# Second-half expert products between first-half outputs, and two more weight buffers, in a fused attention and mixture-of-experts kernel

## The chip, the cores and the metric

The kernel runs on one core of a Trainium2 chip, as one program with one launch. The time is that of the device, in microseconds (us). Each number called "median" is over several executions of the same program; the profile is of one execution of its own. A core has TensorE (PE in the profile, with PEld for its weight loads), VectorE (DVE), ScalarE (ACT), GpSimd (POOL) and SyncE (SP). In this kernel SP issues every transfer between the chip's memory and the on-chip buffers, on one in-order queue, and the transfers run on the core's 16 DMA engines.

## What is computed

Attention with a learned relative-position bias is followed by a soft mixture of experts. The sizes are 8 batches, 8 heads, 576 positions, 64 dims per head; then 4608 tokens of 512 features, 8 experts with 4 slots each, hidden size 1024. All is float32.

```python
# attention: q, k, v are (8, 8, 576, 64)
scores = q @ k^T / sqrt(64) + bias        # bias[h, i, j] = relu(x w1 + b1) @ w2,  x = log1p|i-j| / log1p(max(i, 1))
attn   = softmax(scores)                  # over j
x      = (attn @ v) as (4608, 512)
# mixture of experts
logits     = x @ phi                      # (4608, 32 slots)
slot_input = softmax_over_tokens(logits)^T @ x          # (8 experts, 4 slots, 512)
for e in range(8):
    h = maximum(slot_input[e] @ w1[e], 0)               # w1[e]: 512 x 1024
    slot_out[e] = h @ w2[e]                             # w2[e]: 1024 x 512
out = softmax_over_slots(logits) @ slot_out             # (4608, 512)
```

The expert weights are 8 x 512 x 1024 for w1 and as many for w2. The kernel cuts them into 64 tiles of 512 KB: 32 of w1, then 32 of w2. The result is 9 MB.

## The kernel before

**Main part.** There are 32 units: four pairs of heads (`hp`), and for each pair the eight batches. A bias stage of about 54 us comes first and writes the position bias to memory; each unit then computes scores, softmax and the product with v. In the last pair of heads (units 24 to 31) each unit also does its share of the token mixing (`moe`). The order of all this work is written out by hand: `PLAIN` gives each step of the early units a place, `END` lists the steps from unit 22 on, and every engine runs its instructions in the order in which they were recorded.

**Weights.** `worder` fixes the order of the 64 tiles: tiles 0 to 31 are w1; tiles 32 to 47 are the first half of w2's output columns (`hf` = 0), with two groups `Q` of four experts (32 to 39 and 40 to 47); tiles 48 to 63 are the second half, again with two groups (48 to 55 and 56 to 63). `fetch_w(home)` loads the next tile in this order into a buffer of the pool and tag that is its `home`. The pool `wp` has `W1N` = 24 buffers of 4 KB per partition. During the two middle pairs of heads, each unit fetches one or two tiles into `wp`, by this line:

```python
step(u, "wf", lambda _, u=u: fetch_w((wp, "w"), 2 if u < B + W1N - 2 * B else 1))
```

With B = 8 that is two tiles in units 8 to 15 and one in units 16 to 23, 24 in all. In the last unit, steps named `w21` to `w36` fetch tiles into buffers that attention no longer needs: the bias buffers (`bm`), the query/key buffers (`qk`), the score buffers (`y`), the transposed-attention buffers (`at0`, `at1`), and `v`, `xo`, `xt`, `xk`. After the main part 44 tiles have been asked for. The remaining 20 take over a buffer whose tile has been used; `refetch(i, ...)` asks for the next tiles into the homes of tiles i.

**The end.** After the last unit the code runs straight on, and these are the steps that the change touches:

- `turn_slots` turns the slot inputs, and makes `sel`, two 128 x 128 selection matrices.
- `first(j)`, j = 0 to 7, multiplies the slot inputs by four w1 tiles; `hidden` and `turn_hidden` apply the relu and transpose.
- `second(hf, Q)` multiplies by eight w2 tiles: 32 matmuls (line 888). It holds one of the four pairs of PSUM banks from the call with Q = 0 until the call with Q = 1 has been copied out to `so`.
- `gather_slots(hf)` moves the expert results into the order of the slots (line 899) and copies them to `sst` (line 903).
- `put(hf, b)` makes the output of batch b for half of the columns: four matmuls (line 921) into two bank pairs, one copy on DVE and one on ACT into `ob` (line 315), and a 512 KB transfer by SP (line 924). After every fourth b a rest of 256 KB follows (lines 929, 932, 933).

The order at the end of the code is this, and it is also the order in which PE and SP do it:

```python
gather_slots(0)
for b in range(8):
    put(0, b)
for Q in range(2):
    second(1, Q)
gather_slots(1)
for b in range(8):
    put(1, b)
```

Of the kernel before, what the change touches and what calls it, by code (L numbers as in the profile page):

```python
# [10 lines left out]
F32 = mybir.dt.float32  # L11
F32R = mybir.dt.float32r
AF = mybir.ActivationFunctionType
ALU = mybir.AluOpType
# [2 lines left out]
DRAM = bass.MemoryType.DRAM  # L17


W1N = 24  # L20
W2N = 5
AHEAD = 3
JB0 = 32
# [102 lines left out]
def body(ctx, tc, qk, v, wcol, phi, mw1, mw2, tabh, consth, out, outr):  # L126
    nc = tc.nc
    P = 128
# [8 lines left out]
    const = ctx.enter_context(tc.tile_pool(name="const", bufs=1))  # L137
    dram = ctx.enter_context(tc.tile_pool(name="dram", bufs=1, space=DRAM))
    psp = ctx.enter_context(tc.tile_pool(name="psp", bufs=1, space=PSUM))
    wp = ctx.enter_context(tc.tile_pool(name="wp", bufs=W1N))  # L140
    ldp = ctx.enter_context(tc.tile_pool(name="ldp", bufs=2))
# [3 lines left out]
    xp = ctx.enter_context(tc.tile_pool(name="xp", bufs=1))  # L145
# [16 lines left out]
    rsum = const.tile([P, P], F32, name="rsum")  # L162
# [3 lines left out]
    et2 = xp.tile([P, 256], F32, name="et2", tag="et2")  # L166
# [23 lines left out]
    rowm = cons[:, NJ:]  # L190
# [20 lines left out]
    for g in range(4):  # L211
        rs = slice(32 * g, 32 * g + 32)
        nc.vector.tensor_scalar(out=wbd[rs, H * g:H * g + H], in0=cols[rs, 2:2 + H], scalar1=1.0 / QS, scalar2=None,
                                op0=ALU.mult)
# [99 lines left out]
    def cp(eng, out, in_):  # L314
        (nc.vector.tensor_copy if eng else nc.scalar.copy)(out=out, in_=in_)  # L315
# [22 lines left out]
    def then(u, names, f):  # L338

        place, eng = max(rank[u, n] if (u, n) in rank else (5 * u + PLAIN[n][0], PLAIN[n][1]) for n in names.split())  # L340
        prog.append((place, len(prog), lambda: f(eng)))
# [415 lines left out]
    def fetch_w(home, n=1):  # L757
        for _ in range(n):
            i = nw[0]
            nw[0] += 1  # L760
            w, e, c, hf = worder[i]
            homeof.append(home)
            if not free:
                pool, tag = home
                if tag == "v":
                    free.append([pool.tile([P, 512], F32, name="wt", tag=tag) for _ in range(2)])
                else:
                    x = pool.tile([P, 2, 2, 512] if tag in twice else [P, 1, 2, 512], F32, name="wt", tag=tag)
                    free.extend(x[:, i] for i in range(x.shape[1]))
            wt = free.pop(0)  # L770
            if w == 1:
                nc.sync.dma_start(out=wt, in_=mw1[e, c * P:(c + 1) * P, :].rearrange("p (x d) -> p x d", x=2))
                wt = [wt[:, n, :] for n in range(2)]
            else:
                src = mw2[e, c, hf]
                if type(wt) is list:
                    for n in range(2):
                        nc.sync.dma_start(out=wt[n].rearrange("p (x d) -> p x d", x=2), in_=src[:, 2 * n:2 * n + 2, :])
                else:
                    nc.sync.dma_start(out=wt.rearrange("p y (x d) -> p (y x) d", x=2), in_=src)  # L780
                    wt = [wt[:, n, :] for n in range(2)]
            wtiles[i] = wt
# [12 lines left out]
    for u, (hp, b) in enumerate(units):  # L795
# [9 lines left out]
        if 1 <= hp < NP - 1:  # L805
            step(u, "wf", lambda _, u=u: fetch_w((wp, "w"), 2 if u < B + W1N - 2 * B else 1))
        if u == 1:
# [9 lines left out]
    then(U - 1, "w34 M0.4 M1.4", lambda _: fetch_w((ldp, "v")))  # L817
    then(U - 1, "w34 K01 K23 KR L", lambda _: fetch_w((xp, "xo")))
    then(U - 1, "w34 K01 K23 KR L", lambda _: fetch_w((xp, "xt")))
    sel = [const.tile([P, P], F32, name=f"sel{i}") for i in range(2)]  # L820
    csts, ends, hT2 = {}, {}, {}

    def refetch(*ids):
        for i in ids:
            fetch_w(homeof[i])

    def turn_slots():
        nc.vector.tensor_scalar(out=stS, in0=stS, scalar1=1e-9, scalar2=None, op0=ALU.add)
        nc.vector.reciprocal(out=stS, in_=stS)
        h = Banks()  # L830
        nc.tensor.transpose(out=h.t[:, 0, 0:P], in_=accs, identity=ident)
        sT = ends["sT"] = xp.tile([P, 4, 32], F32, name="sT", tag="ek", bufs=2)
        nc.scalar.copy(out=sT, in_=h.read()[:, 0, 0:P].rearrange("a (c s) -> a c s", c=4))
        for Q in range(2):
            nc.vector.tensor_scalar(out=sel[Q], in0=rsum, scalar1=rowm[:, Q:Q + 1], scalar2=None, op0=ALU.mult)

    def first(j):

        Q, kc = j // 4, j % 4
        if kc == 0:  # L840
            ends["h", Q] = Banks(2)
        for n in range(2):
            for g in range(4):
                nc.tensor.matmul(ends["h", Q].t[32 * g:32 * g + 32, n, :], ends["sT"][:, kc, :], wtiles[4 * j + g][n],
                                 start=kc == 0, stop=kc == 3, tile_position=(0, 32 * g))
# [32 lines left out]
    def second(hf, Q):  # L878

        if Q == 0:  # L880
            ends["o"] = Banks(2)
            ends["so"] = so if hf else wp.tile([P, 2, 512], F32, name="so", tag="w")
        po = ends["o"].t[:, Q, 0:256]
        for fq in range(2):
            for x in range(4):
                for g in range(4):
                    i = 32 + 16 * hf + 8 * Q + 4 * fq + g
                    nc.tensor.matmul(po[32 * g:32 * g + 32], hT2[Q][:, 4 * fq + x, 32 * g:32 * g + 32],  # L888
                                     wtiles[i][x // 2][:, 256 * (x % 2):256 * (x % 2) + 256], start=fq == 0 and x == 0,
                                     stop=fq == 1 and x == 3, tile_position=(0, 32 * g))  # L890
        ends["o"].read()
        cp(Q == 0, ends["so"][:, hf, 256 * Q:256 * Q + 256], po)
        return ends["so"]

    def gather_slots(hf):
        h = Banks()
        pf = h.t[:, 0]
        for Q in range(2):
            nc.tensor.matmul(pf[:, 0:256], sel[Q], so[:, hf, 256 * Q:256 * Q + 256], start=Q == 0, stop=Q == 1)
        h.read()  # L900
        if hf == 0:
            ends["sst"] = wp.tile([P, DM], F32, name="sst", tag="w")
        nc.scalar.copy(out=ends["sst"][:, 256 * hf:256 * hf + 256], in_=pf[:, 0:256])
# [3 lines left out]
    def put(hf, b):  # L907

        sst = ends["sst"][:, 256 * hf:256 * hf + 256]
        pool, tag, n = homes2[8 * hf + b]  # L910
        if n == 0:
            ob = pool.tile([P, 4, 256], F32, name="ob", tag=tag)
        else:
            if n == 1:
                obs[tag] = pool.tile([P, 2, 4, 256], F32, name="ob", tag=tag)
            ob = obs[tag][:, n - 1]
        for z in range(2):
            h = Banks()
            for y in range(2):
                rs = slice(32 * (2 * z + y), 32 * (2 * z + y) + 32)  # L920
                nc.tensor.matmul(h.t[:, y, 0:256], ends["cT"][rs, b, :], sst[rs], start=True, stop=True,  # L921
                                 tile_position=(32 * (2 * z + y), 0))
            cp(z == 0, ob[:, 2 * z:2 * z + 2, :], h.read()[:, :, 0:256])
        nc.sync.dma_start(out=out[b, hf], in_=ob.rearrange("p c d -> p (c d)"))
        if b % 4 == 3:
            h = Banks()
            for r in range(4):
                rs = slice(32 * r, 32 * r + 32)
                nc.tensor.matmul(h.t[64 * (r % 2):64 * (r % 2) + 64, r // 2, 0:256], ends["cR"][rs, b // 4, :], sst[rs],
                                 start=True, stop=True, tile_position=(32 * r, 64 * (r % 2)))  # L930
            obr = wp.tile([P, 2, 256], F32, name="obr", tag="w")
            nc.scalar.copy(out=obr, in_=h.read()[:, :, 0:256])
            nc.sync.dma_start(out=outr[b // 4, hf], in_=obr)
# [4 lines left out]
    with tc.manual_schedule():  # L938
        for _, _, f in sorted(prog, key=lambda x: x[:2]):
            f()  # L940
        turn_slots()
        for j in range(4):
            first(j)
            refetch(*range(4 * j, 4 * j + 4))
        hidden(0)
        first(4)
        first(5)
        turn_hidden(0)
        first(6)
        refetch(24, 25, 27)  # L950
        first(7)
        refetch(28)
        hidden(1)
        so = second(0, 0)
        turn_hidden(1)
        stack(0)
        second(0, 1)
        stack(1)
        gather_slots(0)
        for b in range(8):  # L960
            put(0, b)
        for Q in range(2):
            second(1, Q)
        gather_slots(1)
        for b in range(8):
            put(1, b)

# [61 lines left out]
```

## Time and profile before

| What | Value |
|---|---|
| Median of three runs | 609.73 us (607.46 to 612.27) |
| The profiled execution, its time | 607.81 us |
| The profiled execution, its span from first to last instruction | 605.4 us |
| What lies around the span | 2.4 us |
| Mean granted TensorE clock | 0.993 |
| PE busy | 582.2 us, 96% of the span |
| Moved by DMA | 110.73 MB, 183 GB/s over the span |

The times in the views are microseconds from the start of the span. "Idle before" names what released an engine that had been waiting. A view of windows gives, for each stretch, the busy time of each engine, the granted clock, the share of time that the 16 DMA engines were busy, and what they moved; a share of a little over 1 means that all 16 were busy throughout. An SP row in the view of the timeline shows when transfers were issued, not when their bytes moved. The profile's lines themselves stand in the prediction, where they are used.

### The profile page before, as it was taken

How to read it: one execution, taken by the hardware profiler on the slowest of the kernel's cores; microseconds unless marked ns; L12 is line 12 of the kernel's file. 1: busy time of each engine (PE TensorE's matmuls, PEld its weight loads, DVE VectorE, ACT ScalarE, POOL GpSimd, SP SyncE). 2: the span in 40 equal slices, each digit the busy share in tenths (PEclk: the TensorE clock that was granted, in tenths of full speed). 3: DMA queues.
4: the chain of work that ended last, by engine and by line, in shares of the span. 5: the costliest groups of instructions: out<-in, count | busy, mean ns of one | idle time of the engine just before them, and what ended most of it. 6: DMA issues, size and time to landing. Idle time of an engine off the chain costs nothing.

```text
span 605.4 us, 18911 instructions
## 1 busy us (share of the span) xinstructions
PE 582.2 (96%) x7423; PEld 370.5 (61%) x7423; DVE 414.9 (69%) x1320; ACT 469.8 (78%) x974; POOL 224.6 (37%) x336
## 2 busy tenths in 40 slices
PE   6998899999999999999999999999999999999993
PEld 4874666666666666666666666665666666653551
DVE  7997767667676667667676667677679788852233
ACT  6996888888888888888888888887877887751233
POOL 0001644455555544455555544544233422400000
PEclk9999899999999999999999999999999999999998
DMA  6778222333855544675444356522332145689997
GB/s 223 272 243 298 66 84 84 109 101 123 242 183 190 174 156 154 216 251 175 138 156 138 120 203 222 164 75 73 123 123 71 55 129 210 207 331 324 410 381 316
DMA packets 41897, 110.73 MB, mean 183 GB/s; under 512 B 7120, under 2 KB 7248, under 8 KB 41808
## 3 DMA queue, kind: packets, MB, share of 16 engines
q1 hardware_dynamic: 41808, 109.52, 53.2%
q8 instruction: 58, 0.95, 0.7%
q14 instruction: 31, 0.25, 0.1%
HBM read 82.10 MB, written 27.41 MB: 181 GB/s over the span
## 4 chain that ended last, share of the span: by engine, by line
PE 83%; DMA 6%; DVE 4%; ACT 3%; issue 1%; POOL 0%; SPq 0%; DVEq 0%; ACTq 0%; POOLq 0%
PE ps L473 25%; PE ps L370 21%; PE ps L348 17%; PE ps L260 7%; PE ps L366 6%; DMA wt<-in_moe_w_dram 5%; ACT y L390 2%; PE ps L539 1%; DMA xo<-xs 1%; PE ps L669 1%; PE ps L888 1%; DVE ob L315 1%; PE ps L921 1%; DVE y L383 0%; POOL y L312 0%
## 5 line engine op out<-in xcount | busy, mean ns | idle before, releaser
L312 POOL TENSOR_SCALAR y<-y,sm 128x576 f32<-128x576 f32 (+1 forms) x320 | 221.9, 707 | 302.1 <-DVE sm L399 246.6
L383 DVE CUSTOM_DVE_ANT_0 y<-ps,bm 128x576 f32<-128x576 f32 x256 | 185.3, 754 | 95.5 <-PE ps L348 55.2
L390 ACT ACTIVATE y<-y,mn 128x576 f32<-128x576 f32 x288 | 222.1, 772 | 28.3 <-DVE sm L398 19.3
L315 ACT COPY at<-ps 128x1024 f32<-128x1024 f32 (+3 forms) x211 | 153.9, 732 | 37.0 <-PE ps L348 28.3
L473 PE MATMUL ps<-at,v 128*64 128x320 f32 (+1 forms) x1280 | 176.4, 415 | 0.0
L370 PE MATMUL ps<-qk 64*128 64x288 f32 x1024 | 155.6, 421 | 0.1
L348 PEld LDWEIGHTS ps<-ident,y 64*128 64x128 f32 x2624 | 103.1, 139 | 56.5 <-POOL y L312 16.0
L348 PE MATMUL ps<-ident,y 64*128 64x64 f32 x2624 | 118.0, 226 | 4.1 <-POOL y L312 3.6
L473 PEld LDWEIGHTS ps<-at,v 128*64 128x64 f32 x1280 | 84.0, 137 | 60.7 <-issue 10.8
L370 PEld LDWEIGHTS ps<-qk 64*128 64x128 f32 x1024 | 90.8, 188 | 26.7 <-DVE sm L398 9.8
L390 ACT ACTIVATION_READ_ACCUMULATOR y<-y,mn 128x1 f32 x288 | 53.9, 187 | 0.0
L260 PE MATMUL ps<-f,wbd 128*32 128x79 f32 (+32 forms) x856 | 48.4, 345 | 1.7 <-DVE f L239 1.6
L239 DVE TENSOR_SCALAR f<-tabs,scl,nb 128x576 f32<-128x576 f32 (+17 forms) x114 | 47.9, 496 | 0.5 <-DMA tabs<-in_tab_dram 0.5
L315 DVE COPY at<-ps 128x256 f32<-128x256 f32 (+3 forms) x77 | 33.8, 442 | 15.3 <-PE ps L348 13.8
L260 PEld LDWEIGHTS ps<-f,wbd 128*32 128x32 f32 x856 | 33.2, 112 | 16.9 <-issue 8.1
L366 PE MATMUL ps<-qk 64*64 64x288 f32 x256 | 38.0, 415 | 0.0
L315 DVE COPY xts<-ps 128x256 f32<-128x256 f32 (+1 forms) x57 | 25.9, 455 | 12.1 <-PE ps L473 12.1
L264 ACT ACTIVATE e<-ps,bcon 128x591 f32<-128x591 f32 x36 | 26.7, 754 | 4.7 <-DMA bias_m<-e 2.1
L399 DVE RECIPROCAL sm<-sm 128x2 f32<-128x2 f32 (+1 forms) x160 | 26.5, 165 | 5.5
L398 DVE TENSOR_SCALAR sm<-sm 128x2 f32<-128x2 f32 (+1 forms) x160 | 28.3, 177 | 2.9 <-ACT y L390 2.3
L383 DVE CUSTOM_DVE_ANT_0 y<-ps,br 128x576 f32<-128x576 f32 x32 | 24.0, 750 | 1.9 <-PE ps L348 1.1
L383 DVE DVE_READ_ACCUMULATOR2_ANT mn<- 128x1 f32 x288 | 24.1, 84 | 0.0
(144 smaller groups left out, 333.5 us busy)
## 6 DMA issues: line engine op xcount, KB each, us to landing
wt<-in_moe_w_dram SPq DMA_DIRECT2D x63, 512.0 KB, 6.1
qk<-in_qk_dram SPq DMA_DIRECT2D x32, 608.0 KB, 3.8
v<-in_v_dram SPq DMA_DIRECT2D x32, 320.0 KB, 3.2
bias_m<-e SPq DMA_DIRECT2D x32, 295.5 KB, 4.2
out_dram<-ob SPq DMA_DIRECT2D x16, 512.0 KB, 5.9
xs<-xts SPq DMA_DIRECT2D x24, 288.0 KB, 4.9
xo<-xs SPq DMA_DIRECT2D x8, 864.0 KB, 5.4
bm<-bias_m SPq DMA_DIRECT2D x16, 288.0 KB, 4.4
```

What stands on the lines that cost most here:

```text
L239: nc.vector.tensor_scalar(out=f, in0=tabs[:, 0:n], scalar1=scl[:, sc:sc + 1], scalar2=nb1[:, 0:1], op0=ALU.mult, op1=ALU.max)
L260: nc.tensor.matmul(pb[32 * t:32 * t + 32, c0 // 512, c0 % 512:(c1 - 1) % 512 + 1], wbd, x, start=True, stop=True, tile_position=(0, 32 * t))
L264: nc.scalar.activation(out=e, in_=pb.rearrange("a x n -> a (x n)")[:, 0:S + 15], func=AF.Identity, bias=bc)
L312: nc.gpsimd.tensor_scalar(out=out, in0=y, scalar1=r, scalar2=1.0, op0=ALU.mult, op1=ALU.mult)
L315: (nc.vector.tensor_copy if eng else nc.scalar.copy)(out=out, in_=in_)
L348: nc.tensor.matmul(out, src[rs], ident[rs, rs], is_transpose=True, start=True, stop=True, tile_position=(64 * r, 0))
L366: nc.tensor.matmul(pss[0].t[rs, n, 0:HALF], x[rs, 1152:1216], x[rs, 64 + n * HALF:64 + (n + 1) * HALF], start=True, stop=True, tile_positi ...
L370: nc.tensor.matmul(pss[hh].t[:, n, 0:HALF], x[rs, 640 + p * P:640 + (p + 1) * P], x[rs, k0:k0 + HALF], start=True, stop=True, tile_positio ...
L383: nc.vector.tensor_tensor_reduce(out=d["y", p][:, hs].rearrange("a (x n) -> a x n", x=2), in0=t[:, :, 0:HALF], in1=biases[hp][p][:, hs].re ...
L390: nc.scalar.activation(out=y, in_=y, func=AF.Exp, bias=d["mn", p][:, hh:hh + 1], scale=-1.0, accum_out=d["sm", p][:, hh:hh + 1])
L398: nc.vector.tensor_scalar(out=r, in0=r, scalar1=1e-9, scalar2=None, op0=ALU.add)
L473: nc.tensor.matmul(po[64 * hh:64 * hh + 64], d["v"][:, v0:v0 + 64], main[:, :, 4 * hh + i, :] if i < 4 else rest, start=i == 0, stop=i == ...
```

## The change

`W1N` goes from 24 to 26, so `wp` has two more buffers of 4 KB per partition. By the line above, units 16 and 17 now fetch two tiles each instead of one. Since tiles are taken in a fixed order, each later home holds a tile two places further on. After the main part 46 tiles have been asked for, and 18 are left for `refetch` instead of 20; these now go to the homes of tiles 0 to 13 and 16 to 19, all in `wp`. To make room on chip, `sel` moves from buffers of its own into the buffer `et2`, which the mixing steps no longer use by then.

At the end, the two calls of `second(1, Q)`, and `gather_slots(1)`, move from behind the eight first-half outputs to places between them.

```diff
-W1N = 24
+W1N = 26
...
-    sel = [const.tile([P, P], F32, name=f"sel{i}") for i in range(2)]
...
+        sel = ends["sel"] = xp.tile([P, 2, P], F32, name="sel", tag="et2")
         for Q in range(2):
-            nc.vector.tensor_scalar(out=sel[Q], in0=rsum, scalar1=rowm[:, Q:Q + 1], scalar2=None, op0=ALU.mult)
+            nc.vector.tensor_scalar(out=sel[:, Q], in0=rsum, scalar1=rowm[:, Q:Q + 1], scalar2=None, op0=ALU.mult)
...
-            nc.tensor.matmul(pf[:, 0:256], sel[Q], so[:, hf, 256 * Q:256 * Q + 256], start=Q == 0, stop=Q == 1)
+            nc.tensor.matmul(pf[:, 0:256], ends["sel"][:, Q], so[:, hf, 256 * Q:256 * Q + 256], start=Q == 0, stop=Q == 1)
...
         for j in range(4):
             first(j)
-            refetch(*range(4 * j, 4 * j + 4))
+            refetch(*range(4 * j, 4 * j + (4 if j < 3 else 2)))
         hidden(0)
         first(4)
+        refetch(*range(16, 20))
         first(5)
         turn_hidden(0)
         first(6)
-        refetch(24, 25, 27)
         first(7)
-        refetch(28)
         hidden(1)
...
         gather_slots(0)
-        for b in range(8):
+        for b in range(2):
             put(0, b)
-        for Q in range(2):
-            second(1, Q)
+        second(1, 0)
+        for b in range(2, 4):
+            put(0, b)
+        second(1, 1)
+        for b in range(4, 6):
+            put(0, b)
         gather_slots(1)
+        for b in range(6, 8):
+            put(0, b)
         for b in range(8):
             put(1, b)
```

The first place is PE's queue at the end of the program, from the first output on. `wt` is a weight tile, `hT` the transposed hidden values, `so` the expert results, `sst` the results by slot, `cT` and `cR` the combining weights. Before:

```order
L921 MATMUL ps<-sst,cT 128x256 x16
L929 MATMUL ps<-sst,cR 64x256 x4
L921 MATMUL ps<-sst,cT 128x256 x16
L929 MATMUL ps<-sst,cR 64x256 x4
L888 MATMUL ps<-wt,hT 32x256 x64
L899 MATMUL ps<-so,sel_981 128x256
L899 MATMUL ps<-so,sel_982 128x256
L921 MATMUL ps<-sst,cT 128x256 x16
```

And the same queue with the change, from the same first output:

```order
L921 MATMUL ps<-sst,cT 128x256 x8
L888 MATMUL ps<-wt,hT 32x256 x32
L921 MATMUL ps<-sst,cT 128x256 x8
L929 MATMUL ps<-sst,cR 64x256 x4
L888 MATMUL ps<-wt,hT 32x256 x32
L921 MATMUL ps<-sst,cT 128x256 x8
L899 MATMUL ps<-so,sel 128x256 x2
L921 MATMUL ps<-sst,cT 128x256 x8
L929 MATMUL ps<-sst,cR 64x256 x4
L921 MATMUL ps<-sst,cT 128x256 x16
```

The 64 matmuls of line 888 are split in two and now stand behind the second and the fourth output, the gather stands behind the sixth, and the second half's outputs (the last row) follow straight on the first half's.

The second place is SP's queue in unit 16, in the third pair of heads, and unit 17 has the same edit. `qk` and `v` are the loads for the next unit, and `xs` the store of a unit's result.

```order
 L284 DMA qk<-in_qk_dram 128x1216
 L289 DMA v<-in_v_dram 128x640
-L772 DMA wt<-in_moe_w_dram 128x1024
+L772 DMA wt<-in_moe_w_dram 128x1024 x2
 L485 DMA xs<-xts 128x576
```

One more load of 512 KB stands ahead of the unit's store.

The third place is the end of SP's queue; the rows with `wt` are weight loads, `out_dram` the results.

```order
 L780 DMA wt<-in_moe_w_dram 128x1024 x5
 L778 DMA wt<-in_moe_w_dram 128x512 x2
-L780 DMA wt<-in_moe_w_dram 128x1024 x24
+L780 DMA wt<-in_moe_w_dram 128x1024 x22
 L924 DMA out_dram<-ob 128x1024 x4
 L933 DMA out_dram<-obr 128x512
```

Two loads of 512 KB fewer stand ahead of the first output; the order of the outputs among themselves is the same.

## The prediction

> **What bounds the kernel now.** I read the page first, part 4 (the chain that ended last) and the slices of part 2.
>
> ```profile
> span 605.4 us, 18911 instructions
> PE 582.2 (96%) x7423; PEld 370.5 (61%) x7423; DVE 414.9 (69%) x1320; ACT 469.8 (78%) x974; POOL 224.6 (37%) x336
> ...
> PE   6998899999999999999999999999999999999993
> ...
> DMA  6778222333855544675444356522332145689997
> ...
> PE 83%; DMA 6%; DVE 4%; ACT 3%; issue 1%; POOL 0%; SPq 0%; DVEq 0%; ACTq 0%; POOLq 0%
> ```
>
> PE is busy nearly everywhere and is 83% of the chain. Only in the last five slices, some 75 us, are the DMA engines as busy as PE. The change is at this end, so I cut it into windows next.
>
> ```profile
> core 0: us, PE busy (x) PEld busy (x) DVE busy (x) ACT busy (x) POOL busy (x), PEclk, DMA share, GB/s
> 546.00:550.00 4.00, 3.06 (x29) 0.94 (x32) 2.08 (x10) 0.49 (x2) 0.00 (x0) 1.00 0.79 268
> 550.00:560.00 10.00, 10.00 (x96) 3.48 (x92) 1.44 (x2) 1.27 (x2) 0.00 (x0) 1.00 1.01 364
> 560.00:573.00 13.00, 12.81 (x187) 7.15 (x176) 3.16 (x5) 2.23 (x6) 0.00 (x0) 1.00 1.02 409
> 573.00:581.00 8.00, 6.89 (x89) 3.67 (x93) 5.15 (x8) 5.67 (x11) 0.00 (x0) 1.00 1.03 411
> 581.00:588.00 7.00, 7.00 (x126) 4.06 (x118) 0.42 (x1) 0.59 (x2) 0.00 (x0) 1.00 1.03 413
> 588.00:589.00 1.00, 0.84 (x4) 0.30 (x2) 0.00 (x0) 0.21 (x2) 0.00 (x0) 1.00 0.74 295
> 589.00:590.00 1.00, 0.69 (x12) 0.67 (x16) 0.00 (x0) 0.25 (x1) 0.00 (x0) 1.00 0.41 164
> 590.00:591.00 1.00, 0.55 (x15) 0.15 (x8) 0.85 (x2) 0.89 (x2) 0.00 (x0) 1.00 0.19 74
> 591.00:592.00 1.00, 1.00 (x16) 0.52 (x16) 0.74 (x2) 0.44 (x2) 0.00 (x0) 1.00 0.31 125
> 592.00:603.00 11.00, 4.25 (x52) 2.03 (x48) 3.57 (x6) 4.40 (x8) 0.00 (x0) 0.89 1.01 402
> 603.00:604.00 1.00, 0.00 (x0) 0.00 (x0) 0.00 (x0) 0.00 (x0) 0.00 (x0) 0.50 0.49 188
> ```
>
> From 550 to 588 all 16 DMA engines are busy, at 409 GB/s. Between 588 and 591 they run dry one after another (shares 0.74, 0.41, 0.19): the first is done at 588, the last only at about 591. From 592 they are full again until 603.5. The timeline tells what stands where.
>
> ```profile
> start us, us, engine line op out<-in xcount [idle before <-releaser]
> 573.27 1.15 PE L921 MATMUL ps<-sst,cT 32*128 32x256 f32 x16 [0.46 <-ACT sst L903]
> ...
> 574.83 2.95 SPq L924 DMA_DIRECT2D out_dram<-ob  x4
> ...
> 576.31 0.66 PE L929 MATMUL ps<-sst,cR 32*64 32x256 f32 x8 [0.18 <-DVE ob L315]
> ...
> 576.90 2.86 PE L921 MATMUL ps<-sst,cT 32*128 32x256 f32 x32
> ...
> 580.54 7.11 PE L888 MATMUL ps<-wt,hT 128*32 128x256 f32 x128
> ...
> 587.58 1.26 PE L899 MATMUL ps<-so,sel 128*128 128x256 f32 x4
> ...
> 588.14 0.30 PEld L899 LDWEIGHTS ps<-so,sel 128*128 128x128 f32 x2 [0.26 <-ACT so L315]
> ...
> 589.30 1.15 PE L921 MATMUL ps<-sst,cT 32*128 32x256 f32 x16 [0.46 <-ACT sst L903]
> ...
> 590.91 2.99 SPq L924 DMA_DIRECT2D out_dram<-ob  x4
> ```
>
> So the end has two runners. DMA drains weights, then 4.72 MB of first-half outputs (8 x 524,288 + 2 x 262,144 bytes; 11.5 us at 409 GB/s). PE makes the eight first-half outputs until 580.54, then the second half's products, gather and first output, issued at 590.91. DMA runs dry at about the moment at which PE has new outputs. After that it is DMA alone: 590.91, plus 0.8 until bytes move (row 591 to 592), plus 4.72 MB at 402 GB/s = 11.74, is 603.45, where the rows end (0.49 of the window from 603).
>
> **The change part by part.** *Two more buffers.* Units 16 and 17 each load one more tile.
>
> ```profile
> 273.66 0.57 SPq L772 DMA_DIRECT2D wt<-in_moe_w_dram  x1
> ...
> 287.28 0.42 SPq L772 DMA_DIRECT2D wt<-in_moe_w_dram  x1
> ...
> 280.00:300.00 20.00, 20.00 (x224) 12.52 (x222) 13.56 (x48) 17.55 (x37) 8.78 (x14) 1.00 0.40 122
> ```
>
> Each costs SP about 0.5 us and DMA 1.3 us, where DMA is 0.40 busy and PE, which bounds, is full. What queues behind it on SP is the unit's `xs` store, issued 0.5 us later and read only in the last pair of heads. Cost: 0, covered by PE; if that cover were gone, 2.6 us. At the end, 2 x 524,288 bytes are no longer there to be moved between 550 and 588: at 409 GB/s, DMA is through with the weights 2.56 us earlier. For PE that gains nothing before the first output:
>
> ```profile
> ACT hS L850 <- PE ps L844: 11.5, 2, 8.9
> ...
> PE ps L844 <- ACT sT L833: 0.9, 1, 0.9
> ...
> PEld ps L844 <- DMA wt<-in_moe_w_dram: 0.3, 1, 0.3
> ```
>
> Between 546 and 574 others wait for PE, and PE waited for a weight tile for 0.3 us in all. So the first output still starts at 573.27 (bound of the gain: 0.3 us; I take 0). `sel` in another buffer: the same two DVE instructions at the same place, 0.
>
> In the bias stage the same pool holds features and results, and 26 buffers may spare waits there.
>
> ```profile
> ACT e L264 <- DMA bias_m<-e: 2.1, 2, 1.9
> ...
> 20.00:30.00 10.00, 10.00 (x203) 8.16 (x203) 10.00 (x28) 9.50 (x17) 0.00 (x0) 1.00 0.82 290
> ```
>
> ACT waited 2.1 us for a store to leave a buffer, but PE and DVE are full there, so the gain lies between 0 and 2.1 us; I take 0, since the row with PE and DVE at 10.00 of 10 is the nearer one.
>
> *The reordering.* All of PE's work stays; only its order changes. From 573.27:
> - Outputs 0 and 1: four outputs take 576.31 - 573.27 = 3.04, so two take 1.5: 574.8.
> - Second product, group 0: half of 7.11 = 3.55: 578.35.
> - Outputs 2 and 3 (1.5) and a rest (0.6, from 576.31 to 576.90): 580.45. Now the product holds a bank pair, so three instead of four circulate. PE already waits for copies at outputs:
>
> ```profile
> PEld ps L921 <- DVE ob L315: 3.8, 8, 0.8
> ...
> PEld ps L921 <- ACT sst L903: 1.7, 2, 0.9
> ```
>
>   One such wait more costs 0 to 0.8, mean 0.48 (3.8 over 8); I take 0.3, since part of it overlaps with the rest's matmuls: 580.75.
> - Group 1: 3.55: 584.3. In the end 0.4 to 0.5 us of waiting at `so` and `sst` vanishes, since outputs now stand around the gather.
> - Output 4 is issued 1.6 after its first matmul (590.91 - 589.30): 585.9. Its bytes move at 586.7.
>
> DMA's side of it: the slowest engine ends the first half at 591.0 before, so it ended the weights at 579.5; now at 576.9. Outputs 0 and 1 take 2.56: 579.5. Output 2 is issued at 578.35 + 1.6 = 579.95, moves at 580.75: DMA stands for 1.25. Outputs 2, 3 and a rest, 3.2: 583.95. Then nothing until output 4 at 586.7: DMA stands for 2.75. From there it must move outputs 4 to 7 and a rest (2.36 MB, 5.8) and the second half (11.74). PE keeps ahead of it: gather 1.0, and output 6 is issued at 588.4, the second half's first at about 590.5, both before DMA gets to them (589.3 and 592.5). End: 586.7 + 5.8 + 11.74 = 604.2, against 603.45.
>
> The sum: -2.56 (two tiles) - 0.7 (the old hole, 591.0 to 591.7) + 1.25 + 2.75 (two new holes) = **+0.75 us**. It hangs on one path: PE's work until output 4, since all that lies behind it is DMA at full rate. That makes it robust: had the weights not come earlier, the holes would shrink by as much. On the profiled execution's own span that is 606.15, on its time 608.6. That execution stands 1.9 below the median of the runs; on the median, 609.73 + 0.75 = 610.5.
>
> [...]
>
> By the rows, the reordering fills one hole and opens two, because DMA, at 1.28 us an output, has no reserve of outputs while PE does 3.55 us of products.
>
> **The rivals.** *Faster: no new holes.* If DMA lagged far enough behind, it would stay busy from the weights' end (576.9) for 23.2 us to 600.1. That is 3.3 us less: 606.4. For it speaks that SP's issues in the first half are backed up behind full engines; against it that outputs 2 and 4 cannot be issued before 579.95 and 585.9 by PE's rows.
>
> *Slower: the last weights are late.* PE now asks for tiles 56 to 63 at 580.75 instead of 584.1.
>
> ```profile
> L780 SPq DMA_DIRECT2D wt<-in_moe_w_dram x28: 327/328/1459, 532.5 to 570.4; - x28
> ...
> DMA to landing us min/median/max: 3.7/10.1/12.2
> ```
>
> Before, the last was issued at 570.4 and landed at 580.5 to 582.6; less 2.56 that is 578 to 580, just in time. If it lands no earlier than before, PE stands up to 1.85 us there with every later output behind it: 610.5 + 1.85 = 612.3. It decides from a landing after 580.75 on.
>
> *Faster at the front.* The bias stage gives its 2.1 us: 608.4.
>
> **How the numbers follow.** Forecast 0.55; no new holes 0.2; late weights 0.15; bias stage 0.1. All four lie within 6.1 us of 609.73. The range goes down to the first rival's end and up to the second's, with 0.7 more there because the three runs themselves lie 4.8 us apart: 606.4 to 613.0. Faster or slower by over 1%, about what a measurement of this kernel can tell from no change, means under 603.6 or over 615.8. All gains together (3.3 + 2.1 + 0.3) stay below 6.1 and the slower rival adds 2.6, so I leave 0.03 for each side and 0.94 for within.
>
> **What would show it.** In the changed profile: the last wait for weights gone or unchanged up to 573; the product of line 888 in two pieces, at about 574.8 and 580.75; output issues of the first half in pairs at about 574.8, 580, 586 and 588.4; two dips of the DMA share, near 580 and, deeper, from 584 to 586.7, and none around 590; last bytes at about 604. It would be wrong if PE reached output 4 by 584, or if DMA stayed full through 586, or if the span moved before 546, where nothing but two loads is changed after the bias stage.

## The result and the profile after

| | before | after |
|---|---|---|
| Median, measured in turn | 608.28 us (605.81 to 612.27, 20 runs) | 611.55 us (609.47 to 617.27, 20 runs) |
| Ratio, with its 95% interval | | 1.0062 (1.0041 to 1.0083) |
| The profiled execution, time and span | 607.81 and 605.4 us | 612.70 and 610.9 us |
| Mean granted TensorE clock of that execution | 0.993 | 0.984 |
| First output's first matmul to the end of the span ("tail") | 32.17 us | 34.96 us |

The change made the kernel a little slower in this comparison: 0.4 to 0.8%, which is 2.5 to 5.0 us. (A second comparison of the same two kernels, below, gave 1.0021 with an interval from 0.9988 to 1.0054.) The forecast was +0.75, and 611.55 lies in its range of 606.4 to 613.0.

The page of the changed kernel, the same rows as of the kernel before:

```profile
span 610.9 us, 18917 instructions
...
PE 584.7 (96%) x7423; PEld 373.8 (61%) x7423; DVE 414.3 (68%) x1320; ACT 469.8 (77%) x974; POOL 223.8 (37%) x336
...
PE   6998899999999999999999999999999999989992
...
DMA  6778222334765544676544366531332045699967
...
PE 89%; DVE 4%; ACT 2%; issue 2%; POOL 1%; DMA 1%; SPq 0%; DVEq 0%; POOLq 0%; ACTq 0%
```

The work is the same (PE has 7423 matmuls in both). The last slices differ: PE's last digit was 3 and is 2, DMA's last two were 97 and are 67. DMA has a gap in the second slice from the end, and is still at work in the last one.

The first output now starts at 575.95 instead of 573.27, so 2.68 us came in ahead of the part that the prediction is about, and 34.96 - 32.17 = 2.79 us behind it. The two have different causes. The windows of the start of the program, first of the kernel before:

```profile
50.00:60.00 10.00, 8.19 (x93) 4.69 (x90) 6.07 (x19) 6.16 (x12) 1.47 (x2) 1.00 0.92 335
60.00:70.00 10.00, 8.13 (x92) 5.71 (x90) 8.44 (x29) 8.57 (x18) 5.38 (x10) 0.91 0.34 100
70.00:80.00 10.00, 10.00 (x102) 6.03 (x101) 6.95 (x25) 7.44 (x16) 4.38 (x6) 0.92 0.12 43
```

And of the changed kernel:

```profile
50.00:60.00 10.00, 8.20 (x96) 4.45 (x86) 6.12 (x17) 6.71 (x14) 1.47 (x2) 0.97 1.00 358
60.00:70.00 10.00, 7.89 (x70) 5.27 (x71) 6.27 (x23) 5.99 (x13) 3.37 (x6) 0.67 0.35 105
70.00:80.00 10.00, 10.00 (x114) 6.95 (x112) 7.14 (x25) 8.21 (x17) 6.45 (x10) 0.85 0.01 2
```

The column behind POOL is the granted clock. Between 60 and 70 us it is 0.91 before and 0.67 after, and PE did 92 and 70 matmuls there. In these two traces the clock is either full or half: in the kernel before it was half from 68.2 to 71.6, in the changed one from 59.3 to 66.2 and from 69.6 to 73.0, stretches of 3.4, 6.8 and 3.4 us. In both it is half once more at the end, from 600.7 and from 602.0 on, where PE's last matmul ended at 596.8 and at 599.6. What sets the earlier stretches is not shown: between 50 and 70 us PE's longest pause is 1.8 us in the kernel before and 2.1 in the changed one. That the one profile has one stretch of 3.4 us there and the other three (6.8 us counted as two) is not the change's doing, as the experiments below show.

Behind the first output the path is the one that was forecast. The timeline of the changed kernel (start, duration, engine, line):

```profile
575.95 1.15 PE L921 MATMUL ps<-sst,cT 32*128 32x256 f32 x16 [0.46 <-ACT sst L903]
...
577.50 3.66 PE L888 MATMUL ps<-wt,hT 128*32 128x256 f32 x64 [0.40 <-DVE ob L315]
577.51 6.83 SPq L924 DMA_DIRECT2D out_dram<-ob  x4
...
581.09 1.13 PE L921 MATMUL ps<-sst,cT 32*128 32x256 f32 x12
...
582.64 0.70 PE L921 MATMUL ps<-sst,cT 32*128 32x256 f32 x4 [0.42 <-DVE ob L315]
...
583.86 3.66 PE L888 MATMUL ps<-wt,hT 128*32 128x256 f32 x64
...
584.61 0.33 SPq L933 DMA_DIRECT2D out_dram<-obr  x1
...
587.45 1.26 PE L921 MATMUL ps<-sst,cT 32*128 32x256 f32 x16
...
588.96 3.54 SPq L924 DMA_DIRECT2D out_dram<-ob  x4
```

The product of line 888 stands in two pieces, 1.55 and 7.91 us behind the first output's first matmul (forecast 1.53 and 7.48), and output 4 is issued 13.01 behind it (12.63). Windows of the same stretch; the last two columns are the DMA share and GB/s:

```profile
575.95:577.00 1.05, 1.05 (x16) 0.72 (x16) 0.24 (x1) 0.24 (x1) 0.00 (x0) 1.00 0.43 172
577.00:581.00 4.00, 3.60 (x68) 1.98 (x64) 1.04 (x2) 0.83 (x2) 0.00 (x0) 1.00 0.68 266
581.00:583.00 2.00, 1.58 (x20) 0.99 (x16) 1.53 (x3) 0.59 (x1) 0.00 (x0) 1.00 0.06 25
583.00:587.00 4.00, 4.00 (x72) 2.14 (x72) 0.18 (x1) 1.17 (x2) 0.00 (x0) 1.00 0.82 326
587.00:589.50 2.50, 2.26 (x31) 1.37 (x24) 1.29 (x2) 1.45 (x3) 0.00 (x0) 1.00 0.04 9
589.50:600.00 10.50, 9.23 (x107) 4.87 (x105) 6.45 (x10) 7.61 (x14) 0.00 (x0) 1.00 0.99 391
600.00:606.00 6.00, 0.00 (x0) 0.00 (x0) 0.00 (x0) 0.26 (x1) 0.00 (x0) 0.67 1.02 401
606.00:607.00 1.00, 0.00 (x0) 0.00 (x0) 0.00 (x0) 0.00 (x0) 0.00 (x0) 0.50 0.96 377
```

The two holes are there (share 0.06 and 0.04), and from 589.5 on DMA runs full to the end. A third hole, which the prediction does not have, lies ahead of them (share 0.43 in the first row, and 0.68 in the second). By the trace's records the last weight landed 2.3 us behind the first output's first matmul, against 7.15 in the kernel before; the prediction's sum has 3.6. So from about 576.3 to 578.3, until the first output's bytes move, most engines stand idle. The end has something new too. The window that follows in the changed kernel:

```profile
607.60:609.10 1.50, 0.00 (x0) 0.00 (x0) 0.00 (x0) 0.00 (x0) 0.00 (x0) 0.50 0.07 27
```

For 1.5 us the share is 0.07, and one engine of 16 is 0.0625: fifteen engines are done and one still moves bytes, while the whole kernel waits for it. The window in the same place of the kernel before, whose engines all finish between 603.4 and 603.8:

```profile
603.80:605.40 1.60, 0.00 (x0) 0.00 (x0) 0.00 (x0) 0.00 (x0) 0.00 (x0) 0.50 0.02 5
```

### The profile page after: what moved, and what is told of

It reads as the page before. It is cut to its first block, busy times and chain, and to the rows that moved or that the text cites. A ratio compares the mean times of both kernels' runs of the same rounds, so it can differ in the third digit from the quotient of the medians.

```text
span 610.9 us, 18917 instructions
## 1 busy us (share of the span) xinstructions
PE 584.7 (96%) x7423; PEld 373.8 (61%) x7423; DVE 414.3 (68%) x1320; ACT 469.8 (77%) x974; POOL 223.8 (37%) x336
## 4 chain that ended last, share of the span: by engine, by line
PE 89%; DVE 4%; ACT 2%; issue 2%; POOL 1%; DMA 1%; SPq 0%; DVEq 0%; POOLq 0%; ACTq 0%
PE ps L473 25%; PE ps L370 21%; PE ps L348 17%; PE ps L260 7%; PE ps L366 6%; PE ps L888 2%; PE ps L844 2%; PE ps L539 1%; ACT y L390 1%; PE ps L669 1%; PE ps L921 1%; DVE y L383 1%; DVE ob L315 1%; POOL y L312 1%; DMA tabs<-in_tab_dram 1%
## 5 line engine op out<-in xcount | busy, mean ns | idle before, releaser
L370 PEld LDWEIGHTS ps<-qk 64*128 64x128 f32 x1024 | 92.4, 191 | 26.5 <-DVE sm L398 9.8
L260 PE MATMUL ps<-f,wbd 128*32 128x79 f32 (+31 forms) x856 | 48.4, 348 | 2.2 <-DVE f L239 2.1
L315 DVE COPY at<-ps 128x256 f32<-128x256 f32 (+3 forms) x77 | 33.8, 442 | 16.0 <-PE ps L348 14.7
```

The lines of the kernel that those rows point to most:

```text
L260: nc.tensor.matmul(pb[32 * t:32 * t + 32, c0 // 512, c0 % 512:(c1 - 1) % 512 + 1], wbd, x, start=True, stop=True, tile_position=(0, 32 * t))
L370: nc.tensor.matmul(pss[hh].t[:, n, 0:HALF], x[rs, 640 + p * P:640 + (p + 1) * P], x[rs, k0:k0 + HALF], start=True, stop=True, tile_positio ...
```

## The experiments

All kernels are compared by the tail, from the first matmul of the first output to the end of the span, since what is ahead of it moves with the clock (the first output starts between 572.1 and 579.0 us in these profiles). "Last bytes" and other offsets count from the same matmul. Medians of several runs stand beside it where they were taken.

**Which part of the change costs the time.** One part each, the changed kernel again, and a variant in which the bias stage has its old number of buffers.

The buffers alone, in the old order of the end (`W1N`, `sel` and `refetch` as in the change):

```diff
-W1N = 24
+W1N = 26
```

> The two more buffers alone, with the old order at the end. Theory T (the loss lies in the tail, behind the first output): the DMA engines are through with the weights some 2.5 us earlier, the hole before the second half's first output grows by as much, and the end stays where PE puts it: no change against the kernel before, within 0.5 us; from the first output's first matmul to the end of the span 32.1 us, as before. Theory F (the loss lies in the front: 26 instead of 24 buffers change the bias stage or the clock's start): 1.5 to 3 us slower than before, all of it ahead of 80 us.

Measured: 609.45 us, ratio 1.0019 (0.9987 to 1.0051); tail 32.34, last bytes 30.61 (before 32.17 and 30.49).

The order alone, with 24 buffers:

```diff
         gather_slots(0)
-        for b in range(8):
+        for b in range(2):
+            put(0, b)
+        second(1, 0)
+        for b in range(2, 4):
+            put(0, b)
+        second(1, 1)
+        for b in range(4, 6):
             put(0, b)
-        for Q in range(2):
-            second(1, Q)
         gather_slots(1)
+        for b in range(6, 8):
+            put(0, b)
```

> The new order alone, with 24 buffers and the old loads. Theory T: slower than before by 0.75 us (the step to output 4) up to 2.8 us (what the tail of the changed kernel took more in its profile, 34.95 against 32.13 us from the first output's first matmul), more if group 1's weights are late. Theory F: no more than 0.75 us slower, and nothing moved ahead of 546 us.

Measured: 609.21 us, ratio 1.0005 (0.9966 to 1.0044); tail 34.94.

The changed kernel once more, beside the others:

> The changed kernel once more, for a second profile and its clock. Theory T: the tail from the first output's first matmul is again 34 to 35 us. Theory F: the tail is 33 us, 0.75 over the kernel before, and the first output again starts over 575 us with a granted clock under 0.99. If the shift of the front in the first profile (2.7 us) was the clock's chance, it is gone here.

Measured: 610.38 us, ratio 1.0021 (0.9988 to 1.0054); tail 34.92.

The changed kernel, but with the two new buffers under a tag of their own, so that the pool of the bias stage stays at 24:

```diff
-W1N = 26
+W1N = 24
...
+            if u in (16, 17):
+                step(u, "wf", lambda _: fetch_w((wp, "wx")))
```

> The changed kernel with the two more buffers under a tag of their own, so that the bias stage rotates through 24 as before; loads and order at the end as in the changed kernel. Theory T: as slow as the changed kernel, 3 to 3.5 us over the one before. Theory F: the front's part is gone, 0.75 us over the one before.

Measured: 609.49 us, ratio 0.9997 (0.9965 to 1.0029); tail 34.92.

What follows: the tail separates the kernels without overlap. The old order has 32.17 and 32.34, the new one 34.96, 34.94, 34.92 and 34.92, with 24 or 26 buffers. So by these profiles, one or two of each kernel, the change's cost behind the first output is 2.75 to 2.79 us, all of it the order's, and the buffers give nothing there, as forecast ("had the weights not come earlier, the holes would shrink by as much"). The third hole isn't there in the order alone, with 24 buffers, and the tail is as long. The start of the first output lies anywhere from 572.9 to 579.0 in the four profiles of the new order, and 579.0 is the one with the old number of buffers; with the new buffers and the old order it is 573.1. So the 2.68 us at the front of the changed kernel's profile are not the buffers'.

The times of whole runs do not confirm the 2.75 us. They would be a ratio of 1.0045. The interval of the changed kernel reaches beyond that, but those of the other two new orders end at 1.0044 and 1.0029, a little below. In the kernel before, 35 runs on the chip of these four lie between 605.51 and 617.06, so the chance of the front is larger than the effect. The fastest runs do not settle it either: 605.51 before, but 607.20 with the buffers alone in the old order, and 607.84, 608.76 and 607.87 in the three new orders, each out of a third as many runs. The split of the cost rests on the tails.

**Where the holes come from.** Both products ahead of all outputs, which takes the waiting for PE out of the middle and puts it in one piece at the start:

```diff
         gather_slots(0)
-        for b in range(2):
-            put(0, b)
         second(1, 0)
-        for b in range(2, 4):
-            put(0, b)
         second(1, 1)
-        for b in range(4, 6):
+        for b in range(8):
             put(0, b)
         gather_slots(1)
-        for b in range(6, 8):
-            put(0, b)
```

> Both second products ahead of all first-half outputs, none behind one. Theory L (the end is set by the last output that stands behind the second product of group 1: its issue, 0.9 us to the first bytes, then DMA at full rate for all that follows): the first output is issued 8.7 us after the place where it was issued 1.56 us after; all 23.2 us of outputs follow, so from that place to the end of the span 34.6 us, and 36.2 if a 16 KB instruction load falls into it and one DMA engine ends 1.6 us late, as in the changed kernel. Rival S (splitting the outputs is what costs, each product between them a fixed price): no output is split off, so 32.2, as before.

Measured: 609.90 us in one run. The first output starts later here, so the tail is taken from the gather ahead of it: 36.43, against 33.77 before and 36.51 to 36.55 in the changed kernel. The windows of this kernel show the DMA engines empty while PE makes products and the first output:

```profile
573.00:579.80 6.80, 6.80 (x128) 3.90 (x121) 0.42 (x1) 0.24 (x1) 0.00 (x0) 1.00 0.21 83
579.80:582.00 2.20, 1.96 (x32) 1.25 (x29) 1.29 (x2) 1.45 (x3) 0.00 (x0) 1.00 0.00 0
582.00:606.10 24.10, 12.28 (x142) 6.32 (x140) 9.02 (x14) 10.79 (x19) 0.00 (x0) 0.86 0.99 392
584.80:585.20 0.40, 0.32 (x6) 0.27 (x8) 0.40 (x2) 0.30 (x1) 0.00 (x0) 1.00 0.34 133
```

From 582 on DMA is full but for one short dip (the last row), and no engine ends late. A 16 KB load fell at 582.3, ahead of this dip. In the other kernels the first output starts 1.60 behind the gather, so on the scale of the tail 36.43 is 34.83; counted from the product's first matmul (572.76) it is 35.4. Either is near the 34.6 expected, and the 32.2 falls. The long hole costs 36.43 - 33.77 = 2.66 us, about as much as the holes of the changed kernel and its late engine together.

The products later, behind the fourth and the sixth output, so that DMA has a reserve of outputs while PE multiplies:

```diff
         gather_slots(0)
-        for b in range(2):
+        for b in range(4):
             put(0, b)
         second(1, 0)
-        for b in range(2, 4):
-            put(0, b)
-        second(1, 1)
         for b in range(4, 6):
             put(0, b)
+        second(1, 1)
+        put(0, 6)
         gather_slots(1)
-        for b in range(6, 8):
-            put(0, b)
+        put(0, 7)
```

> The second products behind the fourth and the sixth output, so that two first-half outputs stand behind group 1 instead of four. Theory L: the seventh output is issued 13.8 to 14.2 us after the first output's first matmul, then 3.2 and 11.7 us of transfers: span end at 31.4 to 31.8 us, 0.4 to 0.8 less than before the change; 33.0 to 33.4 with a late DMA engine. Rival S: as in the changed kernel, 34.9, since as many products stand between outputs.

Measured: 609.57 us in one run; tail 34.18, last bytes 32.35. A gain of 0.74 to 0.78 us over the changed kernel, less than the 1.5 to 1.9 expected of the places alone: output 6 is issued 14.50 behind the first matmul, and output 7 only 1.65 later, because the gather stands between. The window in which this shows:

```profile
587.00:589.00 2.00, 2.00 (x24) 1.09 (x20) 0.69 (x1) 1.02 (x3) 0.00 (x0) 1.00 0.05 18
```

**The bank pair.** The prediction gave 0.3 us to the product's hold on one of four bank pairs while outputs 2 and 3 are made. Here each of the two calls takes a pair of its own and gives it back:

```diff
+        if hf or Q == 0:
+            ends["o"] = Banks(1 if hf else 2)
         if Q == 0:
-            ends["o"] = Banks(2)
```

> The changed kernel, but each second product of the second half takes a bank pair of its own and gives it back, instead of one held over the outputs between them. If the held pair is what makes the stretch of outputs 2, 3 and the rest 0.67 us longer than where four pairs circulate: the fifth output is issued at 12.6 instead of 13.0 us after the first output's first matmul, and the tail is 34.5 instead of 34.9 us. If it isn't: 13.0 and 34.9.

Measured: 611.01 us in one run; tail 34.16. The timeline of this kernel, whose lines stand one further down:

```profile
575.07 1.15 PE L922 MATMUL ps<-sst,cT 32*128 32x256 f32 x16 [0.46 <-ACT sst L904]
576.62 3.66 PE L889 MATMUL ps<-wt,hT 128*32 128x256 f32 x64 [0.40 <-DVE ob L315]
580.21 1.32 PE L922 MATMUL ps<-sst,cT 32*128 32x256 f32 x16
581.76 0.66 PE L930 MATMUL ps<-sst,cR 32*64 32x256 f32 x8 [0.23 <-DVE ob L315]
582.35 3.66 PE L889 MATMUL ps<-wt,hT 128*32 128x256 f32 x64
```

Outputs 2 and 3 go through in one piece, where the changed kernel's fourth quarter waited for a copy (its rows at 581.09 and 582.64). The second piece of the product starts 7.28 instead of 7.91 behind the first output, output 4 is issued at 12.38 instead of 13.01, and the tail shrinks by 34.92 - 34.16 = 0.76. The held pair cost 0.63 at output 4, not 0.3.

Both edits together, later products and bank pairs of their own:

> The order of the third run's products (behind the fourth and the sixth output) with bank pairs of their own. Theory L: tail 31.4 us, 33.0 with a late DMA engine; so from 0.7 us faster than the kernel before to 0.9 slower, which the times can hardly tell from no change. Rival S: 34.9, 2.7 us slower.

Measured: 609.80 us, ratio 1.0026 (1.0002 to 1.0050); tail 33.39, last bytes 31.62. Rival S falls, and theory L's 33.0 with a late engine is missed by 0.4. With the pairs freed, the later places give 34.16 - 33.39 = 0.77.

**The late engine.** In all seven profiles with interleaved products up to here one engine ended 1.2 to 1.5 us after the next to last; in the old order, and with the products first, none was late by more than 0.3. The page of the changed kernel has a second kind of DMA beside the program's transfers (queue, kind: packets, MB, share of 16 engines):

```profile
q8 instruction: 59, 0.97, 0.6%
```

These are loads of instructions: 59 of 16,384 bytes are the 0.97 MB. By the trace each is one packet, and behind the first output one takes 0.88 to 1.64 us in the kernel before and the changed one. In the changed kernel the last of them falls at 25.6 us, into the last full stretch, and takes 0.92 us; while it runs, the program's own packets keep 15.2 engines busy, so it takes the place of one engine. In the kernel before, loads fall at 13.1, just ahead of DMA's hole, and then at 33.9, after the end. The load at 25.6 starts 2.3 us after PE has started its last matmul (23.3), so no matmul of the kernel needs it.

Without a change of what is done at the end, the loads can be shifted by making the program longer at its start. Sixty more tiny matmuls, which write the same four numbers again, add 240 instructions to PE's program (the pages count 19157 against 18917). In the changed kernel:

```diff
-    for t in range(4):
+    for r in range(64):
+        t = r % 4
         nc.tensor.matmul(pc[32 * t:32 * t + 32, 0:1], wbd, cols[:, 1:2], start=True, stop=True,
                          tile_position=(0, 32 * t))
```

> The changed kernel, with 60 more tiny matmuls at its very start, which write the same four numbers again; they only shift where in the program the loads of 16 KB of PE's instructions fall, by about 240 instructions. Two theories on the DMA engine that ends 1.4 to 1.6 us after the others in the new order. Theory I: it is late because a 16 KB load falls on it in the last full stretch. If the shift takes the load out of the stretch from 14 to 33 us after the first output's first matmul, no engine is late and the tail falls from 34.9 to about 33.3 us. Rival: the engine is late because the full stretch is longer in the new order, whatever is loaded; then the tail stays at 34.9. If a load still falls into the stretch, both say 34.9 and nothing is told apart. The front gets longer by some 3 to 8 us, which says nothing of the end.

In the kernel before, with 40 more (`range(44)`):

> The kernel before, with 40 more tiny matmuls at its very start, which shift the loads of PE's instructions by about 160 instructions. In the kernel before the loads lie at 13.1 us after the first output's first matmul, in the hole, and at 33.9, after the end; the shift should put one between 18 and 26 us, into the last full stretch. Theory I: one DMA engine is then late by 0.9 to 1.6 us and the tail grows from 32.2 to 33.1 to 33.8 us, in the old order. Rival: no engine is late and the tail stays at 32.2 us. The front gets longer by some 2 to 5 us, which says nothing of the end.

And, since in this one the loads fell at 8.6 and 14.7 us, both ahead of the last full stretch, with 24 more (`range(28)`):

> The kernel before with 24 more tiny matmuls at its start instead of 40. In the last try the loads of 16 KB fell at 8.6 and 14.7 us after the first output's first matmul, ahead of the last full stretch, so nothing was told. With 24 the later one should fall between 18 and 25 us, into the stretch that goes from 18.4 to 30.5. Theory I (a load there holds up one DMA engine): last bytes 0.9 to 1.6 us later than the 30.5 of the kernel before, tail 33.1 to 33.8 instead of 32.2. Rival (only the new order has the late engine): last bytes 30.5, tail 32.2.

Measured, from the trace's records (load: those from 5 us on; last bytes and tail as above):

| Kernel | Order of the end | Loads of 16 KB at | Last bytes | Tail |
|---|---|---|---|---|
| before | old | 13.1, 33.9 | 30.49 | 32.17 |
| with 40 more | old | 8.6, 14.7 | 30.49 | 32.17 |
| with 24 more | old | 10.3, **18.7** | 31.89 | 33.61 |
| after | new | 11.3, **25.6** | 33.19 | 34.96 |
| after, with 60 more | new | 11.1 | 31.81 | 33.54 |

(Times in single runs: 607.43, 609.16 and 608.95 us.) The last windows of the changed kernel with the loads shifted, and then of the kernel before with a load in the stretch:

```profile
603.00:603.70 0.70, 0.00 (x0) 0.00 (x0) 0.00 (x0) 0.00 (x0) 0.00 (x0) 0.50 0.85 325
603.70:605.60 1.90, 0.00 (x0) 0.00 (x0) 0.00 (x0) 0.00 (x0) 0.00 (x0) 0.50 0.02 6
```

```profile
603.00:604.00 1.00, 0.00 (x0) 0.00 (x0) 0.00 (x0) 0.00 (x0) 0.00 (x0) 0.50 0.73 283
604.00:605.40 1.40, 0.00 (x0) 0.00 (x0) 0.00 (x0) 0.00 (x0) 0.00 (x0) 0.50 0.07 29
```

The loads have moved with PE's program, so they are PE's. The share of 0.07 has gone from the one kernel and come to the other. A load in the last full stretch costs 34.96 - 33.54 = 1.42 us in the new order and 33.61 - 32.17 = 1.44 in the old one. That is more than the 0.92 us that the load itself takes in the changed kernel; what makes up the rest is not shown. The rival (a longer full stretch makes an engine late whatever is loaded) would have left both tails where they were; it falls.

Last, the best of the new orders with the loads shifted the same way:

> The kernel with the products behind the fourth and the sixth output and with bank pairs of their own (tail 33.4, of which one late DMA engine 1.4), with the 60 tiny matmuls that took the load out of the last stretch in the changed kernel. Theory I: no late engine, tail 32.0, which is level with the kernel before (32.2); the ratio is then 1.000 within 0.003. Rival: the tail stays at 33.4 and the ratio near 1.002.

Measured: 608.94 us, ratio 1.0009 (0.9989 to 1.0030); tail 32.16, last bytes 30.43. That is the tail of the kernel before (32.17). No version tried beats it.

## Why the prediction was right, and where its sizes were off

*The tail's sum.* The forecast was +0.75 for it, and the profiles say +2.75 to +2.79. The cause of a loss was named rightly: one hole is filled and two are opened, because DMA has no reserve of outputs while PE makes products. What failed are two sizes. That the result lies in the range is partly luck: the range was 6.6 us wide around a forecast of +0.75, and the measured change of +3.27, put on the 609.73 that the forecast started from, gives 613.00, its upper end.

| Part | Forecast | Measured |
|---|---|---|
| Holes, without the held bank pair | +0.45 | 33.54 - 32.17 - 0.76 = +0.6 |
| Held bank pair | +0.3 | +0.76 |
| Last load of instructions in the last stretch | not there | +1.4 |

- *Held bank pair.* The step was "I take 0.3, since part of it overlaps with the rest's matmuls", between 0 and 0.8. It did not overlap: 0.63 of delay at output 4, and 0.76 at the end, once the pair was freed.
- *Late engine.* The prediction ended with bytes divided by the rate of 16 engines, which takes for granted that all 16 end together. It had no term for the kernel's own instruction loads, though the page listed them (58, 0.95 MB), and they decide half of the measured loss. The order moved the last load into the stretch. Why it does so is not settled: PE has as many matmuls and weight loads before as after, and in both kernels the last load comes only after PE's last matmul, at 25.6 in the one and 33.9 in the other. The runs show only that a shift of the program moves it out, and that its place sets the cost.
- *Output 4.* Forecast at 12.63 behind the first output, measured 13.01, and 12.38 with the pair freed, where the forecast without its 0.3 is 12.33. The path by PE's rows up to output 4 and by bytes behind it is right. By the trace's records output 4's bytes began to move at 13.9, and with the loads shifted the last bytes came at 31.81: 17.9 us, where the forecast had 5.8 + 11.74 = 17.5.
- *The weights' end.* The sum had the engines through with the weights at 3.6 us behind the first output; they were at 2.3, and a third hole opened. It cost nothing at the end: with 24 buffers that hole is absent, and the tail is 34.94. This is what the prediction meant by one path, PE's work until output 4.

*The front.* The prediction said that it would be wrong "if the span moved before 546", and the span did move, by 2.68 at the first output. It came with the granted clock between 55 and 78 us, and not with the change: the first output starts at 575.95 and 576.97 in the two profiles of the changed kernel, at 572.10 when its program is 60 matmuls longer, and at 579.02 with the old number of buffers. It goes with the number of half-clock stretches of 3.4 us ahead of it (6.8 us counted as two): 572.1 with none, 572.9 to 575.1 with one, 575.2 to 575.9 with two, 576.0 and 577.0 with three, 579.0 with four. Among these are kernels that differ from the changed one at the end alone, with one stretch and with two. The run's time follows the clock. Of the 20 runs of the changed kernel those with a mean clock of 0.982 took 616.35 to 617.27 us, those with 0.990 or more 609.47 to 612.45. So the agreement of 611.55 with the forecast is in part chance: the second comparison of the same kernel gave a ratio of 1.0021, which is 1.3 us.

*The rivals.* "No new holes" fell: the windows have them. "The last weights are late" fell too; the row of the weight loads and the second piece of the product say so:

```profile
L780 SPq DMA_DIRECT2D wt<-in_moe_w_dram x31: 327/328/1222, 526.4 to 568.2; - x31
...
DMA to landing us min/median/max: 3.8/7.4/11.3
```

The last was issued at 568.2 and landed by 579.5 at the latest (568.2 + 11.3), and PE came to it at 583.86 with no wait. "Faster at the front" fell: ACT waited for its store as before.

```profile
ACT e L264 <- DMA bias_m<-e: 2.3, 4, 1.2
```

And up to the first output PE waited for no weight at all, as forecast (the waits on PE from 546 to 576, complete; the rows of its weight loads, PEld, have no wait for DMA either):

```profile
PE ps L844 <- ACT sT L832: 0.9, 1, 0.9
PE ps L921 <- ACT sst L903: 0.5, 1, 0.5
PE ps L681 <- ACT ek L315: 0.3, 1, 0.3
```

*Interleaving* gives nothing here even with the held pair and the late load taken out: the last kernel ends level with the one before (tail 32.16 against 32.17). Three placings of the products were tried; that no other would gain is not shown.

## What to carry to other kernels

Before putting compute between outputs, count the outputs that are finished and not yet sent: a block of compute that lasts longer than their transfer (here 3.66 us a product; an output takes about 1.28 us, its 524,288 bytes at the 409 GB/s of the window from 560) opened a hole in DMA in each of the three places tried here, and cost about 0.75 us less where it stood later, behind a larger reserve. What a block holds while others run (here one of four bank pairs, 0.76 us) belongs to its price, at full size unless the trace shows the overlap. And where a kernel ends in a stretch with all DMA engines full, look in the trace for the loads of its own instructions there: here one of them on one engine delayed the end by 1.42 to 1.44 us, and 24 more matmuls at the start of the one program brought it in, 60 more in the other took it out.

## What was not expected of the hardware

- One 16 KB load of PE's instructions, 0.92 us on one DMA engine in the changed kernel, delayed the end of the last DMA-bound stretch by about 1.4 us, in either order. In the kernel before it lay outside by luck: 24 tiny matmuls at the start of the program were enough to bring it in.
- The granted clock at the start of the program is not the same in runs of the same code: the half-clock stretches of about 3.4 us come once, up to three times, or (in two profiles) not at all between 55 and 78 us, and in three profiles there are one or two more between 540 and 555. The first output moved between 572.1 and 579.0 us. That is more than the whole effect of the change, so the end of the kernel had to be compared by its own length and not by the run's time.
